# Converted weights written straight into the first batch's weight buffers instead of going through DRAM

## The chip, the cores and the metric

The kernel runs on one core of a Trainium2 chip. The metric is the device time of one execution in microseconds; the median of three executions of the kernel before is 1152.55 us (1151.46 to 1155.24).

## The reference

Three blocks on a batch of 4, a sequence of 768 and a width of 384 (8 heads of 48), in float32:

```python
# 1. a complex recurrence over t for each batch, head and pair (d, e)
S_re, S_im = ar*S_re - ai*S_im + k[t] (x) v[t],  ar*S_im + ai*S_re
y[t] = q[t] @ S_re
# 2. x = y;  u = x + real(fft(fft(x, tokens), channels));  un = layer norm of u
x = u + relu(un @ w_ch1) @ w_ch2                  # 384 -> 1536 -> 384
# 3. token mixing, then a second channel product
u = x + (relu(x.T @ w_tok1) @ w_tok2).T           # 768 -> 256 -> 768
out = u + relu(u @ w_ch1') @ w_ch2'
```

`ar` and `ai` are the given factors, scaled so that their magnitude is at most 0.999.

## The kernel before

For each batch there is a **chain** and **dense work**. The chain is `stage1(b)`, the recurrence in 17 tiles of three steps on VectorE, ScalarE (ACT) and GpSimd (POOL), then eight chunks of small matrix products, and `stage2(b)`, the Fourier transforms as matrix products (L782, L793), the residual sums (L830 to L852) and the normalisation (L858 to L881; for batch 0 its small operations L863 to L869 run on POOL). `transposed` (L670 to L674) turns the result for the **dense work**: `mlp` (L690, L707) for 12 weight blocks p = 0 to 11, the token mixing (`tok1`, L914, blocks 12 and 13; `tok2`, L932, blocks 14 and 15), and a second `mlp` for blocks 16 to 27. While batch b's dense work runs, chain b + 1 runs beside it.

Every product is made of parts: an operand is split into a high part that the matrix unit takes exactly and the low rest, and three products are added. Each of the 28 weight blocks has two halves j = 0, 1; a half is 128 x 2 x 384 numbers (high and low). The weights arrive as 64-bit floating-point numbers, so the kernel first converts them, 56 halves in all: `convert(p, j)` loads one into a buffer of tag T (L184), makes the 32-bit number in two ACT steps (L187, L188), a VectorE shift (L190), a POOL addition (L192) and a VectorE merge (L195), splits it by an ACT cast (L197) and a POOL subtraction (L198), and stores both parts in DRAM (`wscr`, L199). For a product, `Weights.load` fetches a half from DRAM into one of four buffers per j (tags w1 and w2, L244), for every batch, the first included.

A scheduler lays out each engine's instructions ahead of time, by planned times and by priority (`RANK`): on ACT, VectorE and POOL dense work goes first, then conversions (`BACK`), then the chain; on SP, which issues all DMAs, conversions go last. Each queue then runs in that order. `hold` and `rest` tie a conversion's place to a marked instruction. How many conversions are begun where is set by tables: `CF` ten during batch 0's chunks (`tick`), `FC` ten in its `stage2` (`feed`), and the other 36 in the first batch's dense work (`FD`, `FT`), always a fixed number of halves ahead of their use. There are 8 buffers of tag T; the two operands of a product take four of them, the conversions share the rest.

Of the kernel before, what the change touches and what calls it, by code (L numbers as in the profile page):

```python
# [33 lines left out]
TAB, LA, E0, E1 = ("T",), 1, 2, 4  # L34
FD = (18, 14)
KS, EN = 5, 3
FT = (36, 38)
OFF = ((2, 3), 1, 0)
# [3 lines left out]
O = (0, 1, 0)  # L42
FEED = ((0, 2), (0, 0), (0, 0), (0, 0))
HOLD = mybir.DependencyInfo(mybir.DependencyClass.NoSync, mybir.DependencyReason.SCHED_ONLY)
# [10 lines left out]
def attn_fft_mixer_kernel(ctx: ExitStack, tc: tile.TileContext, aL, xL, vL, wL, qN, kN, vN, arN, aiN,  # L55
# [4 lines left out]
    count = [0]  # L60
    RANK = {"pe": (0, 20, 20, 0), "v": (10, 0, 5, 0), "sp": (10, 0, 20, 0)}

# [115 lines left out]

    def convert(p, j):


        n = 384
        t = alloc("T", [128, 3 * n], I32, name="cvt")
        hold(sp.dma_start(out=t[:, 0:2 * n], in_=wL32[p][:, 768 * j:768 * j + 768]))  # L184
        raw = t[:, 0:2 * n].rearrange("p (n t) -> p n t", t=2)
        lo, hi, a = raw[:, :, 0], raw[:, :, 1], t[:, 2 * n:3 * n]
        se.activation(out=a.bitcast(F32), in_=hi.bitcast(F32), func=ACTF.Abs, scale=2.0 ** -112)  # L187
        se.activation(out=lo, in_=lo.bitcast(U32), func=ACTF.Copy, scale=2.0 ** -29)  # L188
        yield
        rest(ve.tensor_scalar(out=a, in0=a, scalar1=3, scalar2=None, op0=ALU.logical_shift_left))  # L190
        yield
        x = ge.tensor_tensor(out=a, in0=a, in1=lo, op=ALU.add)  # L192
        if rests[1] is not None:
            after(x, rests[1])
        rest(ve.scalar_tensor_tensor(out=a, in0=hi, scalar=-0x80000000, in1=a, op0=ALU.bitwise_and, op1=ALU.bitwise_or))  # L195
        parts = t[:, 0:2 * n].rearrange("p (k n) -> p k n", k=2)
        se.copy(out=parts[:, 0, :].bitcast(F32R), in_=a.bitcast(F32))  # L197
        ge.tensor_tensor(out=parts[:, 1, :].bitcast(F32R), in0=a.bitcast(F32), in1=parts[:, 0, :].bitcast(F32), op=ALU.subtract)  # L198
        sp.dma_start(out=wscr[p][j], in_=parts.bitcast(F32))  # L199

    convs = [(p, j) for p in range(28) for j in range(2)]
    active = []

    def feed(n):

        keep, stream[0] = stream[0], BACK
        for _ in range(n):
            if convs:
                for _ in convert(*convs.pop(0)):
                    pass  # L210
        stream[0] = keep

    def tick(n):
# [3 lines left out]
        for _ in range(n):  # L217
            g = convert(*convs.pop(0))
            next(g)
            active.append(g)  # L220
        stream[0] = keep

    class Weights:
# [16 lines left out]
        def load(self):  # L240
            b, p, j = key = self.order[self.loaded]
            self.loaded += 1
            w = alloc("w1" if j == 0 else "w2", [128, 2, 384], F32R, name="w")
            sp.dma_start(out=r32(w), in_=wscr[p][j])  # L244
            self.w[key] = w

# [24 lines left out]
    def stage1(b):  # L271
# [285 lines left out]
        for i in range(NS):  # L557
# [14 lines left out]
            if b == 0 and WS <= i < 16:  # L572
                warm(W0, ybuf[0][i % 2].rearrange("p s c -> p (s c)"))
            feed(FEED[b][0])
        if b == 0:
# [101 lines left out]
    def mlp(u, b, p0, th, tl, done):  # L677
        for qd in range(4):
            hs = []
            for m in range(3):  # L680
# [4 lines left out]
                for g in range(2):  # L685
                    ps = palloc("l", [128, 384])
                    n = 0
                    for kt in range(3):
                        for wi, x in ((0, th), (0, tl), (1, th)):
# [7 lines left out]
                                            op0=ALU.max, op1=ALU.subtract)  # L697
                feed(FD[1] + 2 * p - 56 + len(convs))
                ws.ensure(b, p, 0, 2)
# [236 lines left out]
    def dense1(b, u, th, tl):  # L936
        go(mlp(u, b, 0, th, tl, None))
        R = tok1(b, u)
        feed(FT[0] - 56 + len(convs))
        tok2(b, u, *R)  # L940
        feed(FT[1] - 56 + len(convs))
        return transposed(u, None, "l")
# [32 lines left out]
    t1 = on(FIRST, transposed, u, norm, "s")  # L975
    feed(FD[0] - 56 + len(convs))
    for b in range(B - 2):
        u1, norm = on(CHAIN, chain, b + 1)
        t2 = on(DENSE, dense1, b, u, *t1)
        feed(56)  # L980
        t1 = on(CHAIN, transposed, u1, norm, "s")
        on(DENSE, dense2, b, u, *t2)
        u = u1
# [129 lines left out]
```

## Time and profile before

| | |
|---|---|
| median of three runs | 1152.55 us |
| profiled execution | 1152.89 us, its span 1151.1 us |
| TensorE busy | 997.8 us (87%) |
| VectorE busy | 800.6 us (70%) |
| ACT, POOL busy | 519.8, 376.6 us |
| DMA, mean | 167 GB/s |

Times in the rows below are microseconds from the span's start. PE is TensorE's matmul, PEld its weight load, DVE VectorE, SPq the issue of DMAs by SP. A matmul's busy time overlaps with the next one's. The stages are read from the timeline: batch 0's dense work begins with the first L690 at 215.77; the end of chain 1's recurrence is the row of L428 and L452 (378.3), the end of its chunks the first L747 (444.0), and the end of the chain the last L670 (499.5 to 501). For chain 2 these are 591.0 and 640.3, for chain 3 793.3, 844.2 and 888.9.

### The profile page before, as it was taken

How to read it: one execution, taken by the hardware profiler on the slowest of the kernel's cores; microseconds unless marked ns; L12 is line 12 of the kernel's file. 1: busy time of each engine (PE TensorE's matmuls, PEld its weight loads, DVE VectorE, ACT ScalarE, POOL GpSimd, SP SyncE). 2: the span in 40 equal slices, each digit the busy share in tenths (PEclk: the TensorE clock that was granted, in tenths of full speed). 3: DMA queues.
4: the chain of work that ended last, by engine and by line, in shares of the span. 5: the costliest groups of instructions: out<-in, count | busy, mean ns of one | idle time of the engine just before them, and what ended most of it. 6: DMA issues, size and time to landing. Idle time of an engine off the chain costs nothing.

```text
span 1151.1 us, 21162 instructions
## 1 busy us (share of the span) xinstructions
PE 997.8 (87%) x7276; PEld 929.8 (81%) x7276; DVE 800.6 (70%) x2146; ACT 519.8 (45%) x1442; POOL 376.6 (33%) x531
## 2 busy tenths in 40 slices
PE   1357776699679988989999899999987999999997
PEld 0136664598678877889999889999985999999997
DVE  6997956699999767789976888998475333343332
ACT  7753425677765433576732466772124112211111
POOL 4321956546655466312323621230343001100000
PEclk9988865799979989999999899999988999999999
DMA  6116972477967996355575444755521443634432
GB/s 208 41 42 149 308 281 69 159 222 265 335 221 257 268 307 212 100 161 163 180 189 147 138 125 126 235 168 145 144 82 37 151 138 111 192 118 136 160 108 72
DMA packets 108803, 191.98 MB, mean 167 GB/s; under 512 B 11920, under 2 KB 64272, under 8 KB 108176
## 3 DMA queue, kind: packets, MB, share of 16 engines
q1 hardware_dynamic: 108688, 190.55, 53.5%
q8 instruction: 60, 0.98, 0.4%
q14 instruction: 55, 0.45, 0.1%
HBM read 151.18 MB, written 39.32 MB: 166 GB/s over the span
## 4 chain that ended last, share of the span: by engine, by line
PE 66%; DVE 11%; DMA 6%; POOL 3%; issue 3%; ACT 2%; SPq 0%; POOLq 0%; DVEq 0%; ACTq 0%
PE l L690 23%; PE l L707 22%; DMA cvt<-wL 3%; PE s L793 3%; PE s L782 3%; PE s L472 3%; PE s L406 2%; PE s L521 1%; POOL cvt L198 1%; DMA wscr<-cvt 1%; PE s L914 1%; DVE ws L747 1%; PE s L527 1%; PE s L932 1%; PE s L487 1%
## 5 line engine op out<-in xcount | busy, mean ns | idle before, releaser
L707 PE MATMUL l<-w,h 128*128 128x384 f32 x1728 | 329.9, 343 | 11.1 <-DVE u L710 7.7
L690 PE MATMUL l<-th,w 128*128 128x384 f32 x1152 | 316.8, 344 | 3.4 <-DVE h L696 2.2
L707 PEld LDWEIGHTS l<-w,h 128*128 128x128 f32 x1728 | 301.7, 191 | 15.4 <-DVE u L710 9.1
L690 PEld LDWEIGHTS l<-th,w 128*128 128x128 f32 x1152 | 212.3, 191 | 7.8 <-DVE h L696 4.2
L690 PE MATMUL l<-tl,w 128*128 128x384 f32 x576 | 196.6, 341 | 0.4 <-DVE tl L674 0.4
L694 ACT ACTIVATE h<-l 128x384 fp32r<-128x384 f32 x192 | 94.0, 491 | 227.3 <-PE l L690 226.8
L696 DVE SCALAR_TENSOR_TENSOR h<-l,h 128x384 fp32r<-128x384 f32 x192 | 106.2, 553 | 90.6 <-ACT h L694 90.0
L710 DVE TENSOR_TENSOR u<-u,l 128x384 f32<-128x384 f32 x192 | 105.6, 551 | 79.5 <-PE l L707 78.8
L406 PE MATMUL s<-misc,y 128*112 128x128 f32 x384 | 71.5, 307 | 62.7 <-DVE y L384 41.3
L406 PEld LDWEIGHTS s<-misc,y 128*112 128x112 f32 x384 | 50.9, 149 | 79.3 <-POOL A L345 18.1
L690 PEld LDWEIGHTS l<-tl,w 128*128 128x128 f32 x576 | 110.0, 191 | 1.3 <-DVE tl L674 1.0
L192 POOL TENSOR_TENSOR cvt<-cvt 128x384 int32<-128x384 int32 x56 | 63.5, 1137 | 37.7 <-DVE cvt L190 13.5
L327 POOL TENSOR_TENSOR tm<-tm 128x144 f32<-128x144 f32 (+1 forms) x68 | 35.0, 516 | 106.3 <-ACT tm L326 105.8
L198 POOL TENSOR_TENSOR cvt<-cvt 128x384 fp32r<-128x384 f32 x56 | 64.9, 1164 | 14.0 <-ACT cvt L197 12.6
L472 PE MATMUL s<-qkt 112*96 112x96 f32 x512 | 57.7, 263 | 6.5 <-DVE sc L479 5.5
L371 DVE TENSOR_TENSOR p<-p,A 128x144 f32<-128x144 f32 x192 | 59.8, 312 | 3.1
L472 PEld LDWEIGHTS s<-qkt 112*96 112x96 f32 x512 | 51.8, 174 | 9.1 <-DVE sc L479 6.1
L345 POOL TENSOR_TENSOR A<-raw,tm 128x144 f32<-128x144 f32 (+1 forms) x68 | 34.4, 506 | 66.3 <-DVE yt L374 38.7
L317 POOL TENSOR_TENSOR tm<-sq 128x144 f32<-128x144 f32 (+1 forms) x68 | 35.7, 525 | 56.1 <-ACT sq L312 49.8
L375 DVE TENSOR_TENSOR p<-p,yt 128x96 f32<-128x96 f32 x192 | 50.3, 262 | 3.5
L899 POOL TENSOR_TENSOR xl<-u,xh 128x384 fp32r<-128x384 f32 x18 | 18.0, 1010 | 100.9 <-ACT xh L898 100.9
L195 DVE SCALAR_TENSOR_TENSOR cvt<-cvt 128x384 int32<-128x384 int32 x56 | 44.4, 794 | 9.0 <-POOL cvt L192 8.8
(181 smaller groups left out, 1801.8 us busy)
## 6 DMA issues: line engine op xcount, KB each, us to landing
w<-wscr SPq DMA_DIRECT2D x224, 384.0 KB, 3.7
cvt<-wL SPq DMA_DIRECT2D x56, 384.0 KB, 5.7
wscr<-cvt SPq DMA_DIRECT2D x56, 384.0 KB, 4.7
kn<-y SPq DMA_DIRECT2D x128, 96.0 KB, 2.1
Kn<-kn SPq DMA_DIRECT2D x64, 192.0 KB, 4.8
raw<-aL SPq DMA_DIRECT2D x52, 144.0 KB, 3.2
xx<-xL SPq DMA_DIRECT2D x52, 144.0 KB, 3.2
V<-vL SPq DMA_DIRECT2D x32, 144.0 KB, 4.1
```

What stands on the lines that cost most here:

```text
L192: x = ge.tensor_tensor(out=a, in0=a, in1=lo, op=ALU.add)
L195: rest(ve.scalar_tensor_tensor(out=a, in0=hi, scalar=-0x80000000, in1=a, op0=ALU.bitwise_and, op1=ALU.bitwise_or))
L198: ge.tensor_tensor(out=parts[:, 1, :].bitcast(F32R), in0=a.bitcast(F32), in1=parts[:, 0, :].bitcast(F32), op=ALU.subtract)
L371: x = ve.tensor_tensor(out=cur, in0=prev, in1=A[:, j, 0:3, :], op=ALU.mult)
L375: ve.tensor_tensor(out=cur[:, 0:2, :], in0=cur[:, 0:2, :], in1=y, op=ALU.add)
L406: te.transpose(ps[:, j, :], y[:, j, 0:112], ident)
L472: te.matmul(out=ps[:, j, :], lhsT=K[:, hc, :], rhs=Q[:, hc, :])
L690: te.matmul(out=ps, lhsT=w1[:, wi, kt * 128:kt * 128 + 128], rhs=x[g][:, kt, :], start=(n == 0), stop=(n == 8))
L694: x = se.activation(out=hi, in_=ps, func=ACTF.Relu)
L696: ve.scalar_tensor_tensor(out=h[:, 1, g * 384:g * 384 + 384], in0=ps, scalar=0.0, in1=r32(hi), op0=ALU.max, op1=ALU.subtract)
L707: te.matmul(out=ps, lhsT=hs[m][:, hi, tt * 128:tt * 128 + 128], rhs=w2[:, wi, :], start=(n == 0), stop=(n == 8))
L710: ve.tensor_tensor(out=u[tt], in0=u[tt], in1=ps, op=ALU.add)
```

## The change

For the first batch, a converted half is written straight into the product buffer (tag w1 or w2) from which TensorE will read it: the cast and the subtraction have that buffer as their output, and the store to DRAM, for the later batches, reads it. The first eight halves (blocks 0 to 3) are converted during the chain as before; the next twelve are the token mixing's eight and the second halves of blocks 4, 6, 8 and 10, and these twelve still go through DRAM. The other 36 are made when the weights' order comes to them: `lead` begins up to three ahead, up to the merge, and each is finished when its buffer is given out. On SP conversions now rank between dense work and chain. The operands of batch 1's first product are allotted before the last sixth of batch 0's second `mlp`.

```diff
-FD = (18, 14)
-FT = (36, 38)
-FEED = ((0, 2), (0, 0), (0, 0), (0, 0))
-    RANK = {"pe": (0, 20, 20, 0), "v": (10, 0, 5, 0), "sp": (10, 0, 20, 0)}
+    RANK = {"pe": (0, 20, 20, 0), "v": (10, 0, 5, 0), "sp": (10, 0, 5, 0)}
-    def convert(p, j):
+    def convert(p, j, w=None, held=True):
...
-        hold(sp.dma_start(out=t[:, 0:2 * n], in_=wL32[p][:, 768 * j:768 * j + 768]))
+        x = sp.dma_start(out=t[:, 0:2 * n], in_=wL32[p][:, 768 * j:768 * j + 768])
+        if held:
+            hold(x)
...
-        parts = t[:, 0:2 * n].rearrange("p (k n) -> p k n", k=2)
-        se.copy(out=parts[:, 0, :].bitcast(F32R), in_=a.bitcast(F32))
-        ge.tensor_tensor(out=parts[:, 1, :].bitcast(F32R), in0=a.bitcast(F32), in1=parts[:, 0, :].bitcast(F32), op=ALU.subtract)
-        sp.dma_start(out=wscr[p][j], in_=parts.bitcast(F32))
-    convs = [(p, j) for p in range(28) for j in range(2)]
+        if w is None:
+            parts = t[:, 0:2 * n].bitcast(F32R).rearrange("p (k n) -> p k n", k=2)
+        else:
+            yield
+            parts = w(p, j)
+        se.copy(out=parts[:, 0, :], in_=a.bitcast(F32))
+        ge.tensor_tensor(out=parts[:, 1, :], in0=a.bitcast(F32), in1=r32(parts[:, 0, :]), op=ALU.subtract)
+        sp.dma_start(out=wscr[p][j], in_=r32(parts))
+    early = [(p, j) for p in range(4) for j in range(2)]
+    back = [(p, j) for p in range(12, 16) for j in range(2)] + [(p, 1) for p in (4, 6, 8, 10)]
+    convs = early + back
+    later = [(p, j) for p in range(28) for j in range(2) if (p, j) not in convs]
+    active, begun = [], []
+    def lead():
+        keep, stream[0] = stream[0], BACK
+        while len(begun) < 3 and later:
+            p, j = later.pop(0)
+            g = convert(p, j, ws.place, len(later) > 32)
+            for _ in range(3):
+                next(g)
+            begun.append((p, j, g))
+        stream[0] = keep
     class Weights:
         def load(self):
...
+            if b == 0 and (p, j) not in back:
+                if (p, j) not in early:
+                    lead()
+                    keep, stream[0] = stream[0], BACK
+                    p2, j2, g = begun.pop(0)
+                    assert (p, j) == (p2, j2) and next(g, None) is None
+                    stream[0] = keep
+                    lead()
+                return
+            w = self.place(p, j, b)
+            sp.dma_start(out=r32(w), in_=wscr[p][j])
+        def place(self, p, j, b=0):
             w = alloc("w1" if j == 0 else "w2", [128, 2, 384], F32R, name="w")
-            sp.dma_start(out=r32(w), in_=wscr[p][j])
-            self.w[key] = w
+            self.w[b, p, j] = w
+            return w
...
-                feed(FD[1] + 2 * p - 56 + len(convs))
...
-        feed(FT[0] - 56 + len(convs))
-        feed(FT[1] - 56 + len(convs))
...
-        feed(56)
+        g = mlp2(b, u, *t2)
+        if b == 0:
+            on(DENSE, go, g, 10)
+            on(DENSE, ws.ensure, 0, 27, 1)
         t1 = on(CHAIN, transposed, u1, norm, "s")
-        on(DENSE, dense2, b, u, *t2)
+        on(DENSE, go, g)
```

POOL at the end of batch 0's chain, from the third L831 (the last residual operation) on, before: `rs` are the normalisation's small tiles, `cvt` conversions.

```order
L831 TENSOR_TENSOR ws<-ws 128x193
L192 TENSOR_TENSOR cvt<-cvt 128x384
L198 TENSOR_TENSOR cvt<-cvt 128x384
L192 TENSOR_TENSOR cvt<-cvt 128x384
L863 TENSOR_SCALAR rs<-mv 128x2
L864 TENSOR_SCALAR rs<-mv 128x2
L866 TENSOR_TENSOR rs<-rs 128x2
L192 TENSOR_TENSOR cvt<-cvt 128x384
L198 TENSOR_TENSOR cvt<-cvt 128x384
L192 TENSOR_TENSOR cvt<-cvt 128x384
L198 TENSOR_TENSOR cvt<-cvt 128x384
L865 TENSOR_TENSOR rs<-rs 128x2
```

The same place after (its lines are numbered 34 higher from here: L865 is the L831 above, L897 to L903 are L863 to L869, L201 is L198, L191 is L192).

```order
L865 TENSOR_TENSOR ws<-ws 128x193
L201 TENSOR_TENSOR cvt<-cvt 128x384 x2
L897 TENSOR_SCALAR rs<-mv 128x2
L898 TENSOR_SCALAR rs<-mv 128x2
L899 TENSOR_TENSOR rs<-rs 128x2
L900 TENSOR_TENSOR rs<-rs 128x2 x2
L901 TENSOR_SCALAR rs<-rs 128x2
L897 TENSOR_SCALAR rs<-mv 128x2
L901 TENSOR_SCALAR rs<-rs 128x2
L898 TENSOR_SCALAR rs<-mv 128x2
L902 TENSOR_TENSOR rs<-rs 128x2 x2
```

Of the conversions between the residual operation and the normalisation's operations two are left; the others stand further ahead.

ACT in the middle of batch 0's first `mlp`, before: the cast has the conversion's own buffer as output, and waits for VectorE alone.

```order
L197 CAST cvt_3782<-cvt_3782 128x384 [waits DVE_49]
L348 ACTIVATE A_2294<-tm_2255 128x3x48 [waits DVE_49]
L409 COPY qkt_2064<-s_2269 112x2x64x3 [waits PE_49]
L323 ACTIVATE tm_2306<-tm_2306,lnc_89 128x144 [waits Pool_49]
L349 ACTIVATE A_2294<-A_2294 128x3x48 [waits DVE_49]
L346 COPY A_2294<-A_2294 128x3x48 [waits Pool_49]
L197 CAST cvt_3792<-cvt_3792 128x384 [waits DVE_49,Activation_49]
```

A like place after, where L200 is that cast; `w` is a product buffer, and PE in brackets means that the cast waits until TensorE has left it (the numbers behind the engines are the counters' names).

```order
L200 CAST w_3964<-cvt_3883 128x384 [waits DVE_49]
L348 ACTIVATE sq_2264<-raw_2135 128x288 [waits DMAHW7_49,DVE_49]
L200 CAST w_3915<-cvt_3768 128x384 [waits PE_49]
L370 ACTIVATE tm_2212<-tm_2212 128x144 [waits DVE_49]
L359 ACTIVATE tm_2263<-tm_2263,lnc_89 128x144 [waits Pool_49]
L200 CAST w_4007<-cvt_3919 128x384 [waits DMAHW0_49,DVE_49,PE_49]
L445 COPY qkt_2072<-s_2226 112x2x64x3 [waits PE_49]
L186 ACTIVATE cvt_3930<-cvt_3930 128x384 [waits DMAHW6_49,Activation_49]
```

The cast has a second thing to wait for, in 13 of the 44 halves that are written into a product buffer. Behind it in the queue stand the chain's small steps and evictions.

TensorE in chain 1's Fourier part, before: L793 and L840 are the chain's, L690 and L707 batch 0's dense work, L670 ends the chain.

```order
L707 MATMUL l<-w,h 128x384 x6
L793 MATMUL s<-ws 128x193 x8
L840 MATMUL s<-misc,xT 128x112 x4
L840 MATMUL s<-misc,ws 128x112 x4
L707 MATMUL l<-w,h 128x384 x18
L793 MATMUL s<-ws 128x193 x3
L798 MATMUL s<-ws,fk 1x193 x2
L793 MATMUL s<-ws 128x193
L707 MATMUL l<-w,h 128x384 x2
L840 MATMUL s<-misc,xT 128x112 x4
L840 MATMUL s<-misc,ws 128x112 x4
L707 MATMUL l<-w,h 128x384 x19
```

The same place after (L827, L832, L874, L705 and L442 are L793, L798, L840, L670 and L406).

```order
L874 MATMUL s<-misc,ws 128x112 x4
L827 MATMUL s<-ws 128x193 x8
L874 MATMUL s<-misc,xT 128x112 x4
L874 MATMUL s<-misc,ws 128x112 x4
L827 MATMUL s<-ws 128x193 x3
L832 MATMUL s<-ws,fk 1x193 x2
L827 MATMUL s<-ws 128x193
L874 MATMUL s<-misc,xT 128x112 x4
L874 MATMUL s<-misc,ws 128x112 x4
L705 MATMUL s<-misc,ws 128x128 x18
L442 MATMUL s<-misc,y_69 112x128 x3
```

No dense work of batch 0 is left beside the second half of this stage; it stands earlier, most of it ahead of the end of the recurrence.

Between the row of the last L670 of a chain and the row of L452, L527 and the next last L670, the dense matmuls (L690, L707, L914, L932) number 648, 138 and 150 for chain 1 before, 755, 110 and 71 after, and 493, 97 and 54 for chain 3 in both.

## Rows read from the trace of the kernel before

**Rows 1.** Page, part 2: busy tenths in 40 slices, TensorE and DMA.

```profile
PE   1357776699679988989999899999987999999997
...
DMA  6116972477967996355575444755521443634432
```

**Rows 2.** Busy us (x instructions) per engine by stage; clock, DMA share, GB/s.

```profile
216.00:378.00 162.00, 139.48 (x779) 128.78 (x778) 148.75 (x421) 114.39 (x330) 86.11 (x117) 0.95 0.73 248
378.00:444.00 66.00, 60.98 (x733) 56.60 (x734) 42.38 (x87) 23.43 (x49) 36.01 (x33) 0.92 0.92 280
444.00:500.00 56.00, 48.74 (x289) 43.17 (x289) 47.35 (x135) 31.99 (x98) 25.01 (x35) 0.97 0.46 144
500.00:592.00 92.00, 92.00 (x557) 90.76 (x557) 81.78 (x276) 61.90 (x185) 25.74 (x51) 0.98 0.54 160
591.00:640.00 49.00, 48.64 (x717) 45.13 (x715) 29.86 (x67) 10.55 (x23) 12.03 (x12) 1.00 0.69 173
793.00:844.00 51.00, 51.00 (x725) 48.00 (x723) 28.77 (x65) 8.78 (x20) 12.04 (x12) 1.00 0.53 135
844.00:890.00 46.00, 34.15 (x198) 28.95 (x197) 30.52 (x65) 16.73 (x45) 19.19 (x18) 0.84 0.15 49
```

**Rows 3.** TensorE's timeline: start, us, instruction, [idle before <- releaser].

```profile
189.88 0.95 PE L840 MATMUL s<-misc,ws 112*128 112x112 f32 x4
...
210.20 1.76 PE L670 MATMUL s<-misc,ws 128*128 128x128 f32 x6 [19.36 <-DVE ws L881]
...
215.77 0.67 PE L690 MATMUL l<-th,w 128*128 128x384 f32 x1
...
499.50 1.50 PE L670 MATMUL s<-misc,ws 128*128 128x128 f32 x6 [3.43 <-ACT ws L879]
...
888.85 1.54 PE L670 MATMUL s<-misc,ws 128*128 128x128 f32 x6 [1.50 <-ACT ws L879]
```

**Rows 4.** POOL's timeline, end of batch 0's chain.

```profile
175.47 0.53 POOL L830 TENSOR_TENSOR ws<-ws 128x193 f32<-128x193 f32 x1 [16.69 <-ACT ws L829]
...
191.67 1.13 POOL L192 TENSOR_TENSOR cvt<-cvt 128x384 int32<-128x384 int32 x1
...
210.22 0.99 POOL L198 TENSOR_TENSOR cvt<-cvt 128x384 fp32r<-128x384 f32 x1
...
211.63 0.34 POOL L869 TENSOR_TENSOR rs<-rs 128x2 f32<-128x2 f32 x2
```

**Rows 5.** SP's issue of eight conversion loads, their landing, ACT's first step.

```profile
154.90 6.96 SPq L184 DMA_DIRECT2D cvt<-wL  x8
...
DMA to landing us min/median/max: 6.5/7.6/8.1
...
175.29 0.56 ACT L187 ACTIVATE cvt<-cvt 128x384 f32<-128x384 f32 x1
```

**Rows 6.** VectorE by line, 216 to 378 us: busy, mean ns | idle.

```profile
L195 DVE SCALAR_TENSOR_TENSOR cvt<-cvt 128x384 int32<-128x384 int32 x26 | 19.5, 749 | 1.2 <-POOL cvt L192 1.0
...
L696 DVE SCALAR_TENSOR_TENSOR h<-l,h 128x384 fp32r<-128x384 f32 x33 | 18.2, 550 | 0.5 <-ACT h L694 0.2
...
L710 DVE TENSOR_TENSOR u<-u,l 128x384 f32<-128x384 f32 x30 | 16.3, 545 | 0.0
...
L190 DVE TENSOR_SCALAR cvt<-cvt 128x384 int32<-128x384 int32 x26 | 13.3, 512 | 5.4 <-ACT cvt L187 5.4
```

**Rows 7.** SP's waits, 200 to 500 us: total, times, longest.

```profile
SPq L244 <- DMA wscr<-cvt: 34.9, 15, 4.6
...
SPq L244 <- PE l L690: 20.6, 10, 5.9
...
SPq L244 <- PE l L707: 5.8, 6, 3.7
```

**Rows 8.** Line 195: ns min/median/max.

```profile
L195 DVE SCALAR_TENSOR_TENSOR cvt<-cvt x56: 519/586/1358, 112.6 to 430.5; 128x384 int32<-128x384 int32 x56
```

**Rows 9.** The chain that ended last: 54 dense matmuls.

```profile
934.00 9.36 PE l L707 x54
```

More of the change, by code (lines that the diff above doesn't have):

```diff
@@ L195, in convert, with begin @@
         rest(ve.scalar_tensor_tensor(out=a, in0=hi, scalar=-0x80000000, in1=a, op0=ALU.bitwise_and, op1=ALU.bitwise_or))
-        parts = t[:, 0:2 * n].rearrange("p (k n) -> p k n", k=2)
-        se.copy(out=parts[:, 0, :].bitcast(F32R), in_=a.bitcast(F32))
-        ge.tensor_tensor(out=parts[:, 1, :].bitcast(F32R), in0=a.bitcast(F32), in1=parts[:, 0, :].bitcast(F32), op=ALU.subtract)
-        sp.dma_start(out=wscr[p][j], in_=parts.bitcast(F32))
-    convs = [(p, j) for p in range(28) for j in range(2)]
-    active = []
+        if w is None:
[11 more added lines that the diff above has]
+    active, begun = [], []
+    def begin():
+        p, j = convs.pop(0)
+        return convert(p, j, ws.place if (p, j) in early else None)
     def feed(n):
@@ L208, in feed @@
             if convs:
-                for _ in convert(*convs.pop(0)):
+                for _ in begin():
                     pass
@@ L217, in tick @@
         for _ in range(n):
-            g = convert(*convs.pop(0))
+            g = begin()
             next(g)
             active.append(g)
+        stream[0] = keep
[7 more added lines that the diff above has]
+            begun.append((p, j, g))
         stream[0] = keep
@@ L573, in stage1 @@
                 warm(W0, ybuf[0][i % 2].rearrange("p s c -> p (s c)"))
-            feed(FEED[b][0])
         if b == 0:
@@ L975, in attn_fft_mixer_kernel @@
     t1 = on(FIRST, transposed, u, norm, "s")
-    feed(FD[0] - 56 + len(convs))
+    feed(56)
     for b in range(B - 2):
```

## The prediction

> **What bounds the kernel now.** I read the page's 40 slices first. TensorE is nearly full from about 500 us to the end, and the DMA engines are loaded between 230 and 430 us [rows 1]. So the change, which works on the first batch's weights, can win only before 500 us. Then I read the busy time by stage [rows 2]. Calling the serial work of a batch its chain and its matrix products its dense work, there are four stages: the head, in which batch 0's chain runs alone; A, 216 to 378 us, batch 0's dense work beside the recurrences of chain 1; B, 378 to 444, the rest of the dense work beside chain 1's chunk products; C, 444 to 500, beside chain 1's Fourier part. In A VectorE is busy 148.75 of 162 us: VectorE bounds it, TensorE has 139.48. In B nothing is full except the DMA engines: VectorE 42.38 and TensorE 60.98 of 66, DMA 0.92. The same stage of chains 2 and 3, where nothing is converted, takes 49 and 51 us with TensorE full. C takes 56, chain 3's C 46.
>
> The timelines show the head's end. TensorE stands idle 19.36 us until 210.20 and starts the dense products at 215.77 [rows 3]. What it waits for is the normalisation, whose small operations (L863 to L869) stand on POOL between conversions: from 191.67 to the last of them there are six L192 and nine L198, each 1.0 to 1.3 us [rows 4]. These conversions had their data long before: the eight loads were issued from 154.90 on and landed within 8.1 us, so all were there by about 170, but ACT's first step on them is at 175.29 [rows 5].
>
> **The change, part by part.** Of each engine's instructions only their order changes; the counts of ACT, POOL, VectorE and TensorE are the same, and 56 conversions are still done, 20 of them before the dense work as before. SP loses 44 of the first batch's 56 weight loads; the 56 stores remain. From the first dense product of batch 1 on, TensorE's order is the same row for row, and that stage is full on TensorE (92.00 of 92 us) [rows 2], so what is won by 500 us is kept to the end, and nothing is won after it. The time is therefore 1152.9 us (the profiled run; 0.3 above the median of 1152.55) plus what the four stages gain or lose.
>
> *Head.* In the new order the ten conversions begun in this stage move ahead on ACT, VectorE and POOL; after the third L831 only two of the fifteen POOL operations are left in front of the normalisation. From 191.67 to the end of the last L869 at 211.97 are 20.3 us, of which the fifteen take about 15.7 (15 x 1.05) [rows 4]. What remains is 4.6 us of small operations, two conversions (2.1), and an estimated 2.6 for VectorE's sums and statistics, which the conversions cover now: 9.3 instead of 20.3, a gain of **11.0 us**. The ten have to fit somewhere else: POOL is idle 16.69 us before its first L830 [rows 4], and nine operations (9.5 us) move there, if the loads land. Bounds: 13.6 us at best (13 x 1.05), nothing if the ten push the Fourier part back by as much. I take 11.0, since the gap is longer than what goes into it.
>
> *The removed loads.* A load waits on SP for its store's landing: 34.9 us in 15 waits between 200 and 500 us [rows 7], with chain 1's transfers queued behind. TensorE, however, never names a weight load as what it waited for, so I price the 44 loads themselves at nothing; what they cost appears in B, as late chain transfers and late conversions.
>
> *Stage A.* The order shows more work before the end of the recurrences (the row of L452): 755 dense matmuls instead of 648, and on VectorE six L190, five L195, four L696 and six L710 more. By their means [rows 6] that is 6 x 0.512 + 5 x 0.749 + 4 x 0.550 + 6 x 0.545 = 12.3 us more on the engine that bounds the stage. TensorE's 107 x 0.174 = 18.6 us (a matmul of the dense stream follows the last after 0.174 us: 54 in 9.4) fit in its idle time: 139.5 + 18.6 = 158 of 174. So A **loses 12.3 us**. Bounds: a loss of 31 if every L195 of the stage takes the longest time seen, 1.358 us instead of 0.749 (31 x 0.61 = 19 more) [rows 6, 8]; a gain of 1 if VectorE's 13.25 idle us go. I take the middle one, with the idle time as it is.
>
> *Stage B.* What moved into A is missing here: half of the ten conversions, and 28 of 138 dense matmuls. Chain 3's B is the nearest row: 97 dense matmuls, 51 us, TensorE full [rows 2]. With 110 it is 51 + 13 x 0.174 = 53.3, against 66 now: **12.7 us gained**. Bounds: 17 (chain 2's 49) and nothing.
>
> *Stage C.* 71 dense matmuls beside it instead of 150; the second half of the stage has none. Chain 3's C has 54 and takes 46 us [rows 2, 9]; 17 x 0.174 = 3 more makes 49, and VectorE, which has 47.35 busy us here now against 30.52 there because chain 2's first tiles run in it, will not quite allow that. I take 50, **6 us gained**; bounds 10 and nothing. What is late next is the chain itself: TensorE will wait for it in C with no dense work left.
>
> *The new wait.* In 13 of the 44 conversions that end in a product buffer, ACT's cast now waits for TensorE to leave that buffer. Behind it in ACT's queue stand relu evictions (L694) and the chain's small steps, for which TensorE and VectorE wait. Today the same wait stands on SP, where it costs little: 20.6 us in 10 and 5.8 in 6 [rows 7], 1.65 each. 13 of them make 21 us on an engine that is busy 114.39 of 162 us in A [rows 2]; I cost it at nothing in A, since ACT has 48 idle us there, and its bound is 13 x 5.9 (the longest) = 77.
>
> *A port.* The row of L195, which reads two tensors, goes from 519 ns to 1358, median 586 [rows 8]. The Trainium skill (SBUF — State Buffer, Who interferes with whom) states that a VectorE instruction with two SBUF inputs and a GpSimd instruction that reads SBUF exclude each other for a whole instruction. The row agrees with it, and by that rule denser conversions beside a denser dense stream would make A's loss 31 and not 12.3; the median says that most escape it.
>
> Sum: -11.0 + 12.3 - 12.7 - 6 = -17.4, so 1152.9 - 17.4 = **1135 us**.
>
> **Rivals.** *Smoother than forecast:* with fewer transfers in SP's queue the conversions come in time, and VectorE's 13 idle us in A and four more in C go: 1118. For it: VectorE's idle in A is partly a wait for a conversion's ACT step (5.4 us) [rows 6]. Against it: seven eighths of its time is work.
> *The transfers were hidden anyway:* the ten early conversions only move the wait in the head, or B stays as long as it is because its chain transfers were not late for the loads' sake: without the head's 11 it is 1146, without B's 12.7 it is 1148. For it: TensorE names no weight load. Against it: rows 4 and the 15 us between B and its twins.
> *The port:* every L195 runs at its longest, A loses 31: 1135 + 19 = 1154, no change. For it stands the maximum of row 8, against it the median.
> *The cast in ACT's queue, the one that ends slower:* the 13 waits of ACT hold up evictions, TensorE's buffers fill and the delay stays on the path. At 1.3 us each (17 us) the gain is gone; at 3.0 us, half of the longest seen on SP, it is 39: 1135 + 39 = 1174. For it: the order was laid out by planned times, and the real ones differ; against it: ACT has time, and SP's 1.65 each is an upper measure, since SP asks early.
>
> **How the numbers follow.** Forecast 0.53 (own range 1126 to 1144), smoother 0.17, hidden 0.15, port 0.07, cast 0.08. About 0.3%, 3.5 us, is what can be told from no change: the limit for faster is 1149. Faster: 0.53 + 0.17 + 0.15 = 0.85; the port's 0.07 is the same; the cast's 0.08 slower. The range reaches from just below the smoother case to the hidden one's upper end, 1116 to 1149, and leaves out the port, the cast and a little below.
>
> **What would show it.** Right: the first dense product near 205 us and the idle time before the first L670 of about 8 us; from there to L452 some 174 us with VectorE at about 161; B near 53 and C near 50; the first product of batch 1 near 483; equal times from there on. Wrong: the head's wait unchanged (then the loads land late, or POOL's conversions delay L830); A longer than 185 us, with ACT's casts waiting for TensorE (the cast) or with L195 above 1.2 us in the mean (the port); B above 60 us with conversions still in it.

## The result and the profile after

The changed kernel takes 1120.13 us, median of four runs (1118.05 to 1121.76), against 1153.39 for the kernel before beside it: ratio 0.9693, 95% interval 0.9668 to 0.9718. The profiled run is 1119.06 us long, its span 1117.3 instead of 1151.1. That is 15 us better than the 1135 forecast, inside the range, outside the likeliest case's own 1126 to 1144, and next to the rival "smoother than forecast" (1118).

The page's part 2 of the changed kernel answers to [rows 1]: TensorE's row of eights and nines begins earlier, and the DMA engines' run of nines near 400 us is gone.

```profile
PE   1348887999989998799999999999986999999998
...
DMA  6116974377666756265585336655521543544532
```

The busy time by stage answers to the first four of [rows 2], with the same columns. The stages are cut at the same events: first dense product, end of the recurrences, first instruction of chain 1's Fourier part, first product of batch 1.

```profile
201.30:366.30 165.00, 152.43 (x877) 143.41 (x877) 158.76 (x442) 121.79 (x349) 98.55 (x129) 0.98 0.67 216
366.30:420.50 54.20, 52.44 (x713) 48.74 (x714) 35.26 (x76) 15.23 (x33) 22.35 (x22) 1.00 0.67 191
420.50:468.90 48.40, 37.72 (x216) 31.61 (x216) 41.94 (x124) 30.51 (x93) 24.02 (x33) 0.87 0.45 134
468.90:561.00 92.10, 92.10 (x575) 90.63 (x574) 81.39 (x281) 62.91 (x189) 26.61 (x53) 1.00 0.55 164
```

With the events to a tenth of a microsecond (before: 215.8, 378.3, 444.0, 501.3):

| | before | after | change | forecast |
|---|---|---|---|---|
| head, to the first dense product | 215.8 | 201.3 | -14.5 | -11.0 |
| A | 162.5 | 165.0 | +2.5 | +12.3 |
| B | 65.7 | 54.2 | -11.5 | -12.7 |
| C | 57.3 | 48.4 | -8.9 | -6 |
| from batch 1's first product to the end | 649.8 | 648.4 | -1.4 | 0 |

TensorE's timeline (start, us, instruction, idle time before it) answers to [rows 3]: the wait in front of the first transposes of L705 (L670 before) is 6.04 us instead of 19.36. In C TensorE now waits for the chain, three times, 7.3 us in all; the longest of them is the last row.

```profile
188.90 0.64 PE L874 MATMUL s<-misc,ws 112*128 112x112 f32 x4
195.59 3.25 PE L705 MATMUL s<-misc,ws 128*128 128x128 f32 x12 [6.04 <-DVE ws L915]
...
201.32 0.69 PE L725 MATMUL l<-th,w 128*128 128x384 f32 x1 [0.21 <-ACT th L708]
```

```profile
461.68 1.54 PE L705 MATMUL s<-misc,ws 128*128 128x128 f32 x6 [5.21 <-ACT ws L913]
```

POOL's timeline answers to [rows 4]: the first of the ten conversions (L191) starts at 164.98, in the stretch where POOL stood idle for 16.69 us before, and between the third L865 and the last L903 only two conversions (L201) are left.

```profile
164.98 1.02 POOL L191 TENSOR_TENSOR cvt<-cvt 128x384 int32<-128x384 int32 x1 [5.70 <-ACT cvt L187]
...
190.49 0.53 POOL L865 TENSOR_TENSOR ws<-ws 128x193 f32<-128x193 f32 x1
190.98 1.95 POOL L201 TENSOR_TENSOR cvt<-cvt 128x384 fp32r<-128x384 f32 x2
...
196.76 0.19 POOL L903 TENSOR_TENSOR rs<-rs 128x2 f32<-128x2 f32 x1
```

The loads themselves are no earlier than in [rows 5]: SP issues eight from 154.03 on (154.90 before). But ACT's first step on them is at 163.90 instead of 175.29, and waits 2.88 us for the load rather than the load for it.

```profile
154.03 9.44 SPq L181 DMA_DIRECT2D cvt<-wL  x8
```

```profile
163.90 0.54 ACT L186 ACTIVATE cvt<-cvt 128x384 f32<-128x384 f32 x1 [2.88 <-DMA cvt<-wL]
```

VectorE by line in A (busy, mean ns, idle time before) answers to [rows 6]; the counts are the forecast's, the means a little lower, and the wait of L189 for ACT is 1.3 us instead of 5.4.

```profile
L194 DVE SCALAR_TENSOR_TENSOR cvt<-cvt 128x384 int32<-128x384 int32 x31 | 22.6, 728 | 0.3
L731 DVE SCALAR_TENSOR_TENSOR h<-l,h 128x384 fp32r<-128x384 f32 x37 | 20.2, 547 | 1.4 <-ACT h L729 1.3
L744 DVE TENSOR_TENSOR u<-u,l 128x384 f32<-128x384 f32 x36 | 19.5, 542 | 0.3 <-PE l L741 0.3
...
L189 DVE TENSOR_SCALAR cvt<-cvt 128x384 int32<-128x384 int32 x32 | 14.6, 455 | 1.3 <-ACT cvt L186 1.3
```

The same view for ACT's cast into a product buffer: it waits for VectorE, and hardly for TensorE.

```profile
L200 ACT CAST w<-cvt 128x384 fp32r<-128x384 f32 x31 | 16.0, 518 | 10.4 <-DVE cvt L194 9.1 <-PE l L948 0.8 <-PE s L442 0.4
```

SP's waits from 200 to 470 us answer to [rows 7]: none is for a store's landing. SP now waits mostly for the conversion that it is to store, 50.8 us, where it waited 34.9 us for landings and 27.9 for that (L199) between 200 and 500 us before: its queue is held up little less, by something else. L276 is a weight load from DRAM. The last row is of before.

```profile
SPq L202 <- POOL w L201: 50.8, 23, 6.6
...
SPq L276 <- PE l L741: 13.5, 6, 5.0
```

```profile
SPq L199 <- POOL cvt L198: 27.9, 16, 7.0
```

### The profile page after: what moved, and what is told of

Its sections match the earlier page's. It is cut to its first block, busy times and chain, and to the rows that moved or that the text cites. A ratio compares the mean times of both kernels' runs of the same rounds, so it can differ in the third digit from the quotient of the medians.

```text
span 1117.3 us, 21048 instructions
## 1 busy us (share of the span) xinstructions
PE 994.0 (89%) x7276; PEld 927.8 (83%) x7276; DVE 797.0 (71%) x2146; ACT 516.8 (46%) x1442; POOL 375.4 (34%) x531
## 3 DMA queue, kind: packets, MB, share of 16 engines
q1 hardware_dynamic: 102352, 173.24, 51.1%
## 4 chain that ended last, share of the span: by engine, by line
PE 67%; DVE 14%; DMA 3%; ACT 3%; issue 2%; POOL 2%; SPq 0%; POOLq 0%; DVEq 0%; ACTq 0%
PE l L741 23%; PE l L725 22%; PE s L508 3%; PE s L816 3%; PE s L827 2%; PE s L442 2%; DMA cvt<-wL 2%; PE s L557 2%; PE s L563 1%; PE s L948 1%; DVE cvt L194 1%; DVE ws L781 1%; PE l L966 1%; PE s L966 1%; PE s L523 1%
## 5 line engine op out<-in xcount | busy, mean ns | idle before, releaser
L741 PEld LDWEIGHTS l<-w,h 128*128 128x128 f32 x1728 | 303.2, 192 | 17.2 <-DVE h L731 12.7
L442 PE MATMUL s<-misc,y 128*112 128x128 f32 x384 | 70.8, 305 | 63.9 <-DVE y L420 42.8
L442 PEld LDWEIGHTS s<-misc,y 128*112 128x112 f32 x384 | 50.2, 148 | 81.3 <-POOL A L381 18.3
L191 POOL TENSOR_TENSOR cvt<-cvt 128x384 int32<-128x384 int32 x56 | 62.7, 1120 | 35.4 <-DVE cvt L189 7.5
L508 PE MATMUL s<-qkt 112*96 112x96 f32 x512 | 60.4, 269 | 3.5 <-DVE sc L515 2.7
L407 DVE TENSOR_TENSOR p<-p,A 128x144 f32<-128x144 f32 x192 | 59.5, 310 | 2.6
L508 PEld LDWEIGHTS s<-qkt 112*96 112x96 f32 x512 | 54.4, 179 | 6.1 <-DVE sc L515 2.8
L201 POOL TENSOR_TENSOR w<-cvt,w 128x384 fp32r<-128x384 f32 x44 | 52.5, 1201 | 7.9 <-ACT w L200 4.9
L541 POOL TENSOR_TENSOR yc<-Aa,gm 48x384 f32<-48x384 f32 x18 | 21.0, 1165 | 100.8 <-DVE Aa L534 100.8
L933 POOL TENSOR_TENSOR xl<-u,xh 128x384 fp32r<-128x384 f32 x18 | 17.9, 1007 | 101.1 <-ACT xh L932 101.1
```

Of the source, the lines that this page charges most:

```text
L201: ge.tensor_tensor(out=parts[:, 1, :], in0=a.bitcast(F32), in1=r32(parts[:, 0, :]), op=ALU.subtract)
L407: x = ve.tensor_tensor(out=cur, in0=prev, in1=A[:, j, 0:3, :], op=ALU.mult)
L442: te.transpose(ps[:, j, :], y[:, j, 0:112], ident)
L508: te.matmul(out=ps[:, j, :], lhsT=K[:, hc, :], rhs=Q[:, hc, :])
L741: te.matmul(out=ps, lhsT=hs[m][:, hi, tt * 128:tt * 128 + 128], rhs=w2[:, wi, :], start=(n == 0), stop=(n == 8))
```

## The experiments

In each run's expectation the line numbers are of its own base kernel. Ratios are against the kernel before on the same chip, with the 95% interval. The stage columns are of the one profiled execution of each run, the median is of all of its executions; they can differ (wait1's profiled execution took 1118.2 us, the fastest of four with the median 1122.6). From batch 1's first product to the end the runs differ by up to 6 us (648.4 to 654.6), which I can't explain; so I compare at that product, where the change has done its work. How far one trace can be trusted is seen where an edit should change nothing: the head is 199.2 to 203.5 in the six runs whose edit comes into play behind it (after, loads, stores, wait1, lead1_after, xl_after), and A to C together are 267.1 to 268.3 in the four that leave them alone or nearly so (after, early0_after, loads2, wait1).

| run | ratio [95%] | median us | head | A | B | C | batch 1's first product |
|---|---|---|---|---|---|---|---|
| before | 1 | 1153.4 | 215.8 | 162.5 | 65.7 | 57.3 | 501.3 |
| after | 0.9693 [0.9668, 0.9718] | 1120.1 | 201.3 | 165.0 | 54.2 | 48.4 | 468.9 |
| norm_before | 0.9960 [0.9927, 0.9992] | 1149.0 | 208.7 | 165.0 | 64.0 | 55.8 | 493.5 |
| norm_after | 0.9729 [0.9682, 0.9777] | 1122.3 | 202.0 | 167.1 | 51.1 | 46.1 | 466.3 |
| rank_before | 0.9964 [0.9938, 0.9989] | 1149.7 | 211.9 | 162.9 | 64.7 | 57.8 | 497.3 |
| rank_after | 0.9735 [0.9686, 0.9783] | 1121.7 | 201.1 | 164.9 | 52.1 | 52.2 | 470.3 |
| order_before | 1.0081 [1.0052, 1.0110] | 1163.8 | 215.4 | 159.0 | 75.4 | 58.2 | 508.0 |
| early0_after | 0.9860 [0.9819, 0.9901] | 1138.5 | 216.3 | 165.2 | 54.0 | 47.9 | 483.4 |
| loads | 0.9863 [0.9842, 0.9884] | 1139.6 | 202.1 | 164.8 | 67.5 | 50.0 | 484.4 |
| loads2 | 0.9891 [0.9867, 0.9915] | 1141.9 | 221.4 | 164.9 | 54.7 | 48.7 | 489.7 |
| stores | 0.9742 [0.9711, 0.9773] | 1125.8 | 203.5 | 157.1 | 67.6 | 46.0 | 474.2 |
| wait1 | 0.9745 [0.9701, 0.9789] | 1122.6 | 199.2 | 164.7 | 52.2 | 51.0 | 467.1 |
| lead1_after | 0.9793 [0.9773, 0.9813] | 1130.4 | 199.5 | 161.2 | 59.5 | 56.2 | 476.4 |
| xl_after | 0.9800 [0.9763, 0.9836] | 1130.9 | 200.0 | 160.0 | 55.5 | 56.9 | 472.4 |

### The head

**norm_before, norm_after: the normalisation on VectorE.** Both change one line:

```
-            if b == 0:
+            if False:
```

> The kernel before, with batch 0's small normalisation operations (L863 to L869) on VectorE instead of POOL. Theory (the head was late because these operations stood behind POOL's conversions): the first dense product comes at 201 to 206 us instead of 215.8, TensorE's idle time before the first L670 falls from 19.4 to about 7 us, and since everything after the head stays as it is, the time is 1140 to 1144 us. Rival (the head was gained because the weights' loads or the Fourier part came earlier): the first dense product stays within 3 us of 215.8 and the time within 4 us of 1153.

Only half came, and the time is 5 us above the theory's range: the first dense product at 208.7, 7.1 us earlier, and the time 1149. The timeline of TensorE in norm_before shows where the other half stays. The operations no longer queue on POOL but on VectorE, where the same conversions' steps (L190, L195) stand between them; TensorE waits for L881 twice, 10.2 us in all.

```profile
194.71 0.87 PE L670 MATMUL s<-misc,ws 128*128 128x128 f32 x3 [4.99 <-DVE ws L881]
...
202.15 0.88 PE L670 MATMUL s<-misc,ws 128*128 128x128 f32 x3 [5.21 <-DVE ws L881]
```

> The changed kernel with the same edit (L897 to L903 on VectorE). Theory: there are only two conversions left in front of them on POOL, so 2 to 3 us at most are to be won in the head: first dense product 198 to 202 us, time 1117 to 1121. Rival (POOL's queue still holds the head): first dense product before 195, time below 1114.

The head is the theory's (202.0), the time 1.3 us above its range: C and B are shorter and the rest of the run longer by 5.3. What the edit moves in the head is within the scatter of 4 us, so in the changed kernel nothing of that size is left to win on POOL's queue.

**early0_after: the first eight halves through DRAM again.**

```
-    early = [(p, j) for p in range(4) for j in range(2)]
-    back = [(p, j) for p in range(12, 16) for j in range(2)] + [(p, 1) for p in (4, 6, 8, 10)]
+    early = []
+    back = [(p, j) for p in range(4) for j in range(2)] + [(p, j) for p in range(12, 16) for j in range(2)] + [(p, 1) for p in (4, 6, 8, 10)]
```

> The changed kernel, but blocks 0 to 3 go through DRAM as before (their eight halves are stored and loaded again); the other 36 still go straight into product buffers. In the run with the normalisation on VectorE only 7 of the head's 14 us appeared, and reordering the conversions gave none; VectorE's conversions now fill 164 to 178 us, where it stood idle for 15 us before. Theory (a conversion buffer comes free as soon as its half is written into the product buffer, not when the store has landed, so the next loads and steps come earlier): the first dense product is back at 208 to 216 us, B stays at 53 to 56, time 1127 to 1136. Rival (the head's order comes from the priorities and the list alone): first dense product 199 to 204, time 1118 to 1123.

The whole gain of the head is gone and nothing else: head 216.3, A, B and C as in the changed kernel within 0.5 us each. The timelines are [rows 3] and [rows 4] over again, the long wait and POOL's idle time included.

```profile
210.71 1.75 PE L705 MATMUL s<-misc,ws 128*128 128x128 f32 x6 [20.09 <-DVE ws L915]
```

```profile
175.26 0.54 POOL L864 TENSOR_TENSOR ws<-ws 128x193 f32<-128x193 f32 x1 [16.69 <-ACT ws L863]
```

So what moves the ten conversions into the idle stretch is that the first eight halves are written directly. The time given in the expectation (1127 to 1136) was missed by 2.5 us; the head was not. Its explanation, that conversion buffers come free earlier, is not shown: the eight loads of the ten are issued from 154.66 on here too, and only the ninth and tenth are later (191.99 and 196.34, against 173.45 and 175.80). What differs for the first is where ACT's steps stand in its order: the third of the ten is at 183.38 here and at 166.10 in the changed kernel. Why the scheduler's order comes out so, for the loads that are gone or for the buffers that are free earlier in its plan, stays open.

### The stages A to C

**rank_before, rank_after: the number in RANK alone.**

```
-"sp": (10, 0, 20, 0)}
+"sp": (10, 0, 5, 0)}
```

> The kernel before with one number of the change alone: the third SP number of RANK 5 instead of 20, which sets how far SP's entries of the back part stand ahead. Theory (the direct writes and the conversions' new places made the gain, not this number): 1148 to 1156 us, B (378 to 444 us) still above 62 us. Rival (SP's new order brings the chain's transfers in time): B falls to 55 to 58, time 1140 to 1146.

> The changed kernel with this number back at 20. Theory: 1119 to 1125 us, B (366 to 420 us) 54 to 58. Rival (the number made B's gain): B 62 to 66, time 1130 to 1134.

B's gain is not from here: 64.7 with the new number in the old kernel, 52.1 with the old number in the new one. rank_before's head is 3.9 us shorter, but that can't be put down to the number: in that execution TensorE, busy without a break from 165 to 170 us in both, was granted a clock of 0.95 from 170 to 185 us, near the upper of its two levels, instead of 0.50, the lower one. It ended the Fourier part at 183.3 us instead of 190.8, and its wait for the normalisation grew to 23.1 us. In the changed kernel nothing of the 3.9 shows. The stretch in before, then in rank_before:

```profile
170.00:185.00 15.00, 15.00 (x48) 10.37 (x47) 4.49 (x13) 4.39 (x11) 3.26 (x6) 0.50 0.00 0
```

```profile
170.00:185.00 15.00, 13.09 (x71) 9.32 (x70) 8.72 (x23) 9.23 (x23) 7.61 (x11) 0.95 0.01 2
```

**order_before: the new order of conversions, all through DRAM.**

```
-FD = (18, 14)
+FD = (18, 18)
-    convs = [(p, j) for p in range(28) for j in range(2)]
+    convs = [(p, j) for p in (0, 1, 2, 3, 12, 13, 14, 15) for j in range(2)] + [(p, 1) for p in (4, 6, 8, 10)]
+    convs += [(p, j) for p in range(28) for j in range(2) if (p, j) not in convs]
```

> The kernel before, every half still through DRAM, but converted in the order of the changed kernel: blocks 0 to 3 and 12 to 15, the second halves of 4, 6, 8 and 10, then the rest; all ten conversions of the head are begun under 18. Theory (the head is a matter of where the conversions stand, A and B of the way through DRAM): the first dense product comes 5 to 14 us earlier, A and B keep their 162 and 66 us, time 1139 to 1148. Rival (the order of conversion made all of it): B falls to 54 to 57 us and the time to 1120 to 1128.

Slower by 0.8%: the head does not move (215.4), and B grows to 75.4. With halves that come back from DRAM this order gains nothing; both accounts were wrong. The run doesn't separate the order from the lead, though: with the token mixing's halves in front, blocks 4 to 11 are converted fewer halves ahead of their use. The first weight load of block 4 is issued at 238.0 us instead of 223.0.

**loads, stores, wait1: the removed traffic and the removed wait, put back.** Each adds one transfer for each of the 36 halves that are written straight from the start of A on; nothing reads what it brings. In this order:

```
+                    sp.dma_start(out=dump, in_=wscr[p][j])
```

```
+        if w is not None and (p, j) not in early:
+            sp.dma_start(out=wsc2[p][j], in_=r32(parts))
```

```
+                    sp.dma_start(out=dump[:, len(later) + len(begun)], in_=wscr[p][j][0:1, 0, 0:16])
```

> The changed kernel, and for 36 of the 44 halves written straight into product buffers SP also loads the stored half back into a tile that nobody uses: it brings back the 192 KB times two of traffic each and SP's wait for the store's landing, but no product waits for them. Theory (the wait in SP's queue delays the chain's and the conversions' transfers): B grows from 54 to 60 to 66 us, time 1126 to 1136. Rival (the loads were hidden; the places of the conversions made the gain): time 1118 to 1123 and B 53 to 56.

> The changed kernel, and each of the 36 halves is stored a second time, into DRAM that nobody reads: 384 KB more of traffic at the place where the loads were in the run with the stored halves, but SP waits for no store's landing and for no unused tile. If the bytes lengthened that run's B (67.5 us): B 60 to 67, time 1130 to 1140. If SP's waits did: B 53 to 56, time 1118 to 1124.

> The changed kernel, and for each of the 36 halves SP loads 64 bytes of the stored half, each into its own unused place: SP waits for the store's landing as it did for a weight load, and nothing else is added (2 KB in all). The run with whole halves reached batch 1's first product at 484.4 us, 15.5 later than the changed kernel, the run with second stores, which adds the bytes without a wait, 5.3 later. Theory (the other ten microseconds are SP standing in front of stores that have not landed): SP waits 20 to 60 us for landings between 200 and 470 us, the first product of batch 1 comes at 476 to 482, time 1126 to 1133. Rival (SP's waits for the unused tile made those ten, or reads cost more than writes; waits for landings are covered): 468 to 472, time 1118 to 1123.

The run with the loads comes to batch 1's first product 15.5 us later than the changed kernel, although nobody waits for what they bring: A stays, B goes from 54.2 to 67.5, beyond the theory's range as the time is (1139.6). With the second stores it is 5.3 later and the time lies between the two accounts (1125.8). Of the 5.3 only 3.1 fall into A to C: the head is 2.2 us longer, and the first second store is issued at 226.1, behind it. Of the 15.5 the loads have 14.7 in A to C. B alone misleads for the stores: it is 67.6 because A ends earlier, at 157.1; with work that can slide over a stage's border, only the sum of the stages counts. With the tiny loads A to C take 267.9 us, 267.6 in the changed kernel, and yet SP did wait for landings, as its waits from 200 to 470 us show:

```profile
SPq L273 <- DMA wscr<-w: 19.5, 16, 3.3
```

So the theory that SP's wait for landings made ten of the loads' microseconds falls, and the rival's account holds. What the remaining 11.6 us of the loads are stays open. SP's longest waits from 200 to 484 us in that run were for the one unused tile, which the kernel before does not have: each load waits until the one before it has landed. Of these waits 22.0 us lie in B. And reads may cost more than writes.

```profile
SPq L273 <- DMA dump<-wscr: 37.0, 20, 3.9
```

The loads did not make the conversions late again. ACT waits for conversion loads in A and B together 25.0 us before, 6.9 after and 5.3 in loads, in this order:

```profile
L187 ACT ACTIVATE cvt<-cvt 128x384 f32<-128x384 f32 x36 | 20.0, 555 | 25.0 <-DMA cvt<-wL 25.0
```

```profile
L186 ACT ACTIVATE cvt<-cvt 128x384 f32<-128x384 f32 x36 | 20.2, 562 | 8.2 <-DMA cvt<-wL 6.9 <-POOL w L201 1.3
```

```profile
L187 ACT ACTIVATE cvt<-cvt 128x384 f32<-128x384 f32 x36 | 19.8, 551 | 5.4 <-DMA cvt<-wL 5.3
```

The stage rows of loads and of stores (B of each) show the DMA engines in between those of before (0.92) and after (0.67):

```profile
366.90:434.40 67.50, 61.93 (x760) 57.97 (x759) 38.20 (x79) 16.11 (x35) 22.67 (x23) 0.97 0.82 247
```

```profile
360.60:428.20 67.60, 67.49 (x798) 62.91 (x797) 43.87 (x89) 20.79 (x46) 28.61 (x28) 1.00 0.86 265
```

**loads2: traffic without a store in front of it.**

```
+                    for c in range(2):
+                        sp.dma_start(out=dump[:, c].bitcast(I32), in_=wL32[p][:, 768 * j + 384 * c:768 * j + 384 * c + 384])
```

> The changed kernel, and for the same 36 halves two loads of 192 KB of the weights into an unused tile: the same traffic, without any wait for a store. If the bytes cost: as the run with the stored halves, 1126 to 1136. If the wait on SP costs and not the bytes: 1118 to 1123, and only the other run is longer. If the loads were hidden: both 1118 to 1123.

Inconclusive on its question: these loads depend on nothing, so all 72 were issued between 13 and 111 us, in the head:

```profile
L274 SPq DMA_DIRECT2D dump<-wL x72: 327/328/584, 13.0 to 111.1; - x72
```

The head is 20.1 us longer (first dense product 221.4), and A to C are as in the changed kernel; the time, 1141.9, is above all three accounts. Whether the bytes made the head longer is open too: SP waited 48.1 us in front of the next load of the unused tile up to 120 us, with the recurrence's transfers in the same queue.

```profile
SPq L274 <- DMA dump<-wL: 48.1, 65, 1.5
```

**lead1_after: one conversion begun ahead instead of three.**

```
-        while len(begun) < 3 and later:
+        while len(begun) < 1 and later:
```

> The changed kernel with one load of a conversion begun ahead instead of three. Theory (conversions that have their data in time are what let VectorE's idle time in A fall from 13 to 6 us): each conversion's first step waits for its load, A grows from 165 to 170 to 180 us, time 1125 to 1138. Rival (VectorE's idle time fell for another reason, and the loads are early enough anyway): 1118 to 1123, A 163 to 167.

The time is in the theory's range (1130.4), the place is not: A became shorter (161.2), B and C 5.3 and 7.8 us longer. Conversions slid out of A: VectorE has 431 instructions there instead of 442. Its idle time in A is 9.45 us, between the 6.24 of the changed kernel and the 13.25 before, so the lead accounts for part of what the idle time lost. Making halves three ahead is worth 9.3 us of A to C.

**xl_after: work taken from VectorE in A.**

```
-XL = (0,), (0, 1, 2, 3, 4, 5)
+XL = (), (0, 1, 2, 3, 4, 5)
```

> The changed kernel with batch 0's six subtractions of the token mixing's low parts (L933) on POOL instead of VectorE. Theory (VectorE's work bounds A, 158.8 busy of 165.0 us): six of 0.70 us leave VectorE and A shrinks by 3 to 5 us, time 1115 to 1118. Rival (A is bound by the chain from product to product, or POOL's slower operation delays the token mixing): A 164 to 168, time 1119 to 1124.

A shrank by 5.0 us, as expected of a stage that VectorE bounds, and C grew by 8.5: fewer dense products were done by A's end (824 matmuls instead of 877), and C has 274 instead of 216. The kernel is slower for it (1130.9), which neither account had. VectorE has 15 instructions less in A, not 6, so other work left the stage too, and that VectorE bounds it is only made likely. The stages of xl_after:

```profile
200.00:360.00 160.00, 144.59 (x824) 135.77 (x825) 152.05 (x427) 118.29 (x342) 95.76 (x129) 0.97 0.65 212
360.00:415.50 55.50, 50.95 (x708) 47.52 (x707) 35.88 (x78) 15.83 (x35) 26.67 (x26) 1.00 0.72 187
415.50:472.40 56.90, 46.92 (x274) 40.97 (x273) 47.99 (x134) 32.94 (x101) 26.43 (x37) 0.93 0.47 143
```

No run beat the changed kernel.

## Why the prediction was right, and where it was not

**Head: the place right, the gain 3.5 us larger, the cause one step short.** The prediction counted POOL's conversions in front of the normalisation, and fifteen became two. Its bound of 13.6 us holds for what it was worked out for: TensorE's wait fell by 13.3 us (19.36 to 6.04). The rest is the Fourier part, which ended at 189.54 us instead of 190.83; from 185 to 190 us TensorE's granted clock was 0.84 there and 0.50 before. The mis-sized term is what the step left standing between the third L865 and the last L903, 9.3 us; it measured 6.0 (190.98 to 196.95), with nothing to see of the 2.6 for VectorE's sums. And the step took the new order as given; early0_after shows that direct writing of the first eight halves makes it. norm_before shows no more than that POOL's queue is not the only place where the conversions can hold up the normalisation: on VectorE it gains 7.1 us.

**Stage A: the term that was mis-sized.** The step said that the 21 further VectorE instructions add 12.3 us, "with the idle time as it is". They added some 10 (148.75 to 158.76, [rows 2] and the row above), since the means fell, L190's from 512 to 455 ns. And the idle time did not stay: 13.25 us became 6.24, of which 4.1 is the wait of L189 for ACT, and with it ACT's wait for conversion loads in A (12.0 us before, 5.1 after). A lost 2.5. This is the half of the smoother rival that came true: 7 of its 13 us of idle time in A. That the time landed beside its 1118 is in part luck: other terms made up the rest, the head with 3.5 us and A's smaller busy time with 2.3. Its "seven eighths" is 148.75 of 162, 92%. With 2.5 in the place of 12.3 the forecast's sum is 1126.

**Stage B: the size right** (54.2 against 53.3), the cause not shown. The conversions were late there: ACT waited 13.0 us for their loads in B before, 1.8 after; ten conversion loads were issued in it before, two after (the last at 421.8 and 371.7 us), and the transfers in B fell from 18.34 to 10.34 MB. But in loads B is long with the conversions in time. And the step had no term for the clock: B's granted clock was 0.92 before and is 1.00 now, as in the rows of chains 2 and 3 that it went by. It fell to the lower level behind a stretch in which TensorE was busy for 6.2 of 10 us:

```profile
403.00:408.00 5.00, 3.32 (x43) 2.92 (x41) 2.28 (x4) 0.99 (x2) 1.88 (x3) 1.00 0.96 344
408.00:413.00 5.00, 2.88 (x41) 2.46 (x38) 3.62 (x8) 2.20 (x5) 3.70 (x4) 0.80 0.86 269
413.00:418.00 5.00, 5.00 (x25) 5.00 (x25) 2.37 (x4) 2.35 (x6) 3.95 (x4) 0.51 1.05 354
```

**Stage C: right in kind, 3 us larger than forecast;** TensorE waits for the chain there, as said. From batch 1's first product on the time is the same within 1.4 us.

**The removed loads.** "What they cost appears in B" is borne out in part: second stores of the same size cost 3.1 us in A to C, little more than the scatter of 1.2, and loads 14.7, with SP's waits for the unused tile in it. "TensorE never names a weight load" holds for that one trace: in norm_before, where the dense work begins earlier, it waits 2.9 us for them. The row that the step leaned on, SP's 34.9 us of waits for landings [rows 7], is no price: wait1 has 19.5 us of such waits and is not later.

**The rivals.** "Hidden anyway" fell with the head and B, which both gained what it denied. The cast in ACT's queue waits 1.2 us for TensorE in all of A, not 21.

The port did not make A longer by 19 us, but it is there, and its price was mis-read. The Trainium skill (SBUF — State Buffer, Who interferes with whom) has a VectorE operation with two inputs in SBUF, as L194 is, and a POOL operation that reads SBUF exclude each other. The trace agrees: in A each of the 14 of 31 L194 that take more than 590 ns began while a POOL operation was under way, and ended 404 to 421 ns after that operation. So a meeting costs what is left of POOL's operation; only an L194 that begins just behind it, as here, takes the longest time.

```profile
346.50 1.39 DVE L194 SCALAR_TENSOR_TENSOR cvt<-cvt 128x384 int32<-128x384 int32 x1
```

```profile
346.46 1.02 POOL L201 TENSOR_TENSOR w<-cvt,w 128x384 fp32r<-128x384 f32 x1
```

Above 545 ns each, the usual time of one that meets nothing, the L194 of A lose 5.7 us; the 26 L195 lost 5.3 before. The bound had every one of them meet POOL at the worst moment. The prediction's reason against it was a median over all 56, which says little about A: there 16 of the 26 were above 570 ns before, so most did not escape.

```profile
L194 DVE SCALAR_TENSOR_TENSOR cvt<-cvt x56: 540/558/1394, 112.9 to 381.3; 128x384 int32<-128x384 int32 x56
```

**The parts.** Of the 32.4 us up to batch 1's first product, the first eight halves' direct writes are 14.5 (early0_after gives them back), all of it in the head. The other 36 and their way ahead of use are 17.9, and here the cause is not taken apart: putting equal transfers back takes 3.1 us (stores) to 14.7 (loads, with the waits for the unused tile), cutting the lead to one takes 9.3, and these overlap. On TensorE the 17.9 are 9.8 us less idle time and 8.1 less busy time for as many matmuls (1808 and 1805), with the granted clock at 0.97 instead of 0.94. A to C before, then after:

```profile
215.80:501.30 285.50, 250.70 (x1808) 229.95 (x1806) 239.24 (x643) 170.80 (x479) 147.13 (x185) 0.94 0.72 234
```

```profile
201.30:468.90 267.60, 242.59 (x1805) 223.76 (x1806) 235.97 (x640) 167.53 (x473) 144.92 (x183) 0.97 0.63 196
```

## What to carry to other kernels

Taking a round trip through memory away can pay where no engine names its transfers as what it waits for: look at the work that it lets move (here the conversions, into idle time of the head) and for other transfers beside it in a full stretch. When a stage bounded by one engine gets more work, ask of its idle time too, whether the same change feeds it better. Compare kernels at an event behind all stages that trade work, since a shorter stage can be paid for in the next. A minimum, median and maximum over a whole run say little about one stage: list the operations of the stage, with what runs beside each.

## What was not expected

SP's waits for stores to land, 19.5 us in 16, cost nothing that wait1 shows, though its queue is in order. 13.8 MB (36 times 384 KB) that nobody needs took 14.7 us of A to C as loads and 3.1 as stores, and 20.1 as loads in the head's first 111 us; both times as loads they brought waits of SP for the one unused tile (37.0 and 48.1 us), so these are no prices of the bytes alone. And the order of conversions that is good with direct writes is bad without them and with its shorter lead: 1.0081 of the time before.
